# TensorE's program as a loop over heads, with K and V rings of one head each, in a single-query attention kernel

## The chip, the cores and the metric

One core of a Trainium2 chip. The metric is device time in microseconds (us), the median of several executions. The kernel before takes 336.5 us. "Span" is the profiled execution from its first to its last instruction; the times are 1.7 to 2.6 us longer.

## The reference

Attention of one query per head over a long sequence: 16 heads, 8192 keys, head size 256, bfloat16.

```python
B, H, Sq, Sk, D = 1, 16, 1, 8192, 256
scores = jnp.einsum("bhqd,bhkd->bhqk", q, k) * D ** -0.5
p = softmax(scores)
out = jnp.einsum("bhqk,bhkd->bhqd", p, v)
```

K and V are 134 MB and are read once. One head's K is loaded in two halves of 2 MB (32 columns of 128 keys each), and so is its V.

## The kernel before

SyncE issues all loads. K halves go to a ring of 6 buffers, V halves to a ring of 4. Of the 32 columns of a K half, VectorE multiplies 24 with the query (one multiply-and-sum each); TensorE transposes and multiplies the other 8. After a head's two K halves VectorE finds the maximum, ScalarE computes the exponents E, and TensorE multiplies E with V ("PV", 16 matmuls per V half).

The order of the loads: four K halves first, then V and K in turn, so the last K half is followed by four V halves.

```python
items = [("k", *kx) for kx in kseq[:K_LEAD]]            # K_LEAD = 4
rest_k, vseq = kseq[K_LEAD:], list(kseq)
while rest_k or vseq:
    if vseq:   items.append(("v", *vseq.pop(0)))
    if rest_k: items.append(("k", *rest_k.pop(0)))
# [cut] each load waits until its buffer is free:
if n >= slots:                                          # 6 for K, 4 for V
    waits = [f"{kind}free{n - slots}"] + ([f"ktfree{n - slots}"] if kind == "k" else [])
```

A K buffer is free when VectorE has done its 24 columns (`kfree`) and TensorE its 8 (`ktfree`); a V buffer when its PV is done (`vfree`). VectorE does the global maximum of the head before (`xmax`) after the tenth column of the next head's first K half, so E and PV of a head come only then:

```python
for n, (h, x) in enumerate(kseq):
    for c in range(DVE_COLS):                           # 24
        dve(... tensor_tensor_reduce(prod, Kb[slot][c], qb[h], accum_out=S[:, col]) ...)
        if x == 0 and h >= 1 and c == 9: xmax(h - 1)
        if x == 1 and h >= 1 and c == 9: rcp(h - 1)
    if x == 1: dve(... m[h] = max(S of head h) ...)
```

Every engine's program is emitted straight, 16 heads one after the other. Nine tiny loads named `scr`, before the last V half, are a measuring aid; nobody reads what they load.

## Time and profile before

| | before |
|---|---|
| time, median (range) | 336.5 us (336.39 to 336.52, 3 runs) |
| span | 334.8 us |
| DMA, slices 2 to 37 of 40 | 90% or more busy |
| VectorE, one K half | 8.7 us |
| DMA, one half | 4.9 us |
| one head: DMA / VectorE | 19.6 us / 17.4 us |

From the page of the kernel before: the span; the busy tenths of DMA in 40 slices of the span and the GB/s in each; the DMA queues that carry instructions (packets, MB, share of 16 engines' span); the loads with the median time from issue to landing.

```profile
span 334.8 us, 5443 instructions
...
DMA  7999999999999999999999999999999999999910
GB/s 255 430 429 429 430 425 426 429 429 422 431 427 419 433 431 424 425 431 424 423 435 428 423 427 430 423 427 432 425 423 432 431 419 430 433 419 425 377 66 12
...
q8 instruction: 13, 0.21, 0.3%
q14 instruction: 16, 0.13, 0.1%
...
Kb<-in_k_dram SPq DMA_DIRECT2D x31, 2048.0 KB, 39.0
Vb<-in_v_dram SPq DMA_DIRECT2D x31, 2048.0 KB, 34.4
...
```

DMA has 9 in nearly every slice, near 430 GB/s (419 to 435 from the second to the 37th): it bounds the kernel. A load lands 34 to 39 us after its issue, so seven or eight are queued at any time. The page also lists two queues of kind "instruction": q8 with 13 packets of 16,384 bytes, which took 0.98 to 1.11 us each, and q14 with 16 packets.

The trace holds more. In it each load's semaphore gets 16 increments, one by one: those of the last K half come from 296.98 to 309.83 us. They are read here as 16 parts of the load, and "ring" is the name given to what brings one part. Worked out from those moments for the kernel before (us; "step" is the time from the last increment of the load before):

```
load              1st ring   15th ring   16th (last)   step of last
k half  ..           96.36       99.07       100.40        4.89
  ..                101.24      103.97       106.31        5.91
  ..                106.18      108.86       111.16        4.85
  ..                120.86      124.51       125.85        4.86
  ..                130.60      134.29       136.61        5.87
last K half         296.98      301.24       309.83        5.84
V half 28           301.87      306.12       314.77        4.95
V half 30           311.64      315.95       324.51        4.83
```

The first ring keeps a step of about 4.89 us throughout. The last one has a step of 5.7 to 5.9 eleven times between 55 and 310 us and so ends 12.9 us behind the first and 8.6 behind the fifteenth. (The trace doesn't name the rings: 1st to 16th is the order in which they arrive. That the 16th is one and the same ring is inferred from its lag behind the first, which grows step by step; at 208 us it is already 5.3 us behind the fifteenth.) The engines start with the 16th increment: V half 28 has it at 314.77 and its PV starts at 314.82, V half 30 at 324.51 and 324.56. So the last ring sets the time of everything.

TensorE's timeline at the end (start, duration, operation, [idle before it]):

```profile
...
314.82 5.23 PE L471 MATMUL acc<-Vb,E 128*2 128x512 bf16 x16 [0.82 <-DMA Vb<-in_v_dram]
319.88 0.38 PE L413 MATMUL misc<-ident,m 128*1 128x128 f32 x2
320.10 1.89 PE L471 MATMUL acc<-Vb,E 128*2 128x512 bf16 x8
...
322.23 1.89 PE L471 MATMUL acc<-Vb,E 128*2 128x512 bf16 x8
...
324.56 1.03 PE L471 MATMUL acc<-Vb,E 128*1 128x256 bf16 x8 [0.41 <-DMA Vb<-in_v_dram]
...
326.47 6.28 PE L471 MATMUL acc<-Vb,E 128*1 128x256 bf16 x56
```

PV of V half 28 (314.82), the maximum of the last head (319.88), two parts of PV 29 with the last head's softmax between, and then PV 30 and 31 in single rows (324.56 to 332.8).

### The profile page before, as it was taken

The page shows a single profiled execution, that of the slowest core. Times are in us where ns is not written, and L with a number is a line of the kernel's source. Part 1 is how long each engine was busy: PE and PEld are TensorE (multiplying, and loading weights), DVE is VectorE, ACT ScalarE, POOL GpSimd, SP SyncE. Part 2 cuts the span into 40 slices and gives each one's busy share as a digit, 9 for nine tenths or more (in the row PEclk, how much of TensorE's full clock was granted, in tenths as well). Part 3 has the DMA queues.
Part 4 walks back from the last instruction along what each step waited for, and adds up shares of the span by engine and source line. Part 5 has one row for each costly group of instructions (what it writes and reads, how often), then busy time and mean ns, then how long its engine had stood idle before and what let it go on. Part 6 is the DMA issues. An engine that isn't in the chain of part 4 may idle for free.

```text
span 334.8 us, 5443 instructions
## 1 busy us (share of the span) xinstructions
PE 246.3 (74%) x1742; PEld 112.2 (34%) x1742; DVE 281.6 (84%) x1619; ACT 94.3 (28%) x170; POOL 0.2 (0%) x4
## 2 busy tenths in 40 slices
PE   1455857877887877697778688777788776887797
PEld 0433323333332423333233232333333333332335
DVE  7799999799998989787899797998787989797910
ACT  2253204333231324313143321333213333221310
POOL 0000000000000000000000000000000000000000
PEclk9999969799877969869698987779877789877799
DMA  7999999999999999999999999999999999999910
GB/s 255 430 429 429 430 425 426 429 429 422 431 427 419 433 431 424 425 431 424 423 435 428 423 427 430 423 427 432 425 423 432 431 419 430 433 419 425 377 66 12
DMA packets 10289, 134.59 MB, mean 402 GB/s; under 512 B 1282, under 2 KB 1299, under 8 KB 2068
## 3 DMA queue, kind: packets, MB, share of 16 engines
q1 hardware_dynamic: 10224, 134.23, 95.0%
q8 instruction: 13, 0.21, 0.3%
q14 instruction: 16, 0.13, 0.1%
q10 hardware_dynamic: 36, 0.02, 0.0%
HBM read 134.23 MB, written 0.01 MB: 401 GB/s over the span
## 4 chain that ended last, share of the span: by engine, by line
DMA 56%; PE 22%; DVE 16%; ACT 4%; issue 1%; SPq 1%; DVEq 0%
DMA Vb<-in_v_dram 29%; DMA Kb<-in_k_dram 27%; PE acc L471 18%; DVE prod L265 15%; ACT KT L372 2%; PE acc L492 2%; PE tp L363 1%; ACT ac L486 1%; SPq L227 1%; PE misc L423 1%; ACT E L437 1%; DVE S L265 0%; PE spe L388 0%; DVE g L239 0%; PE tp L316 0%
## 5 line engine op out<-in xcount | busy, mean ns | idle before, releaser
L265 DVE CUSTOM_DVE_ANT_0 prod<-Kb,qb 128x256 bf16<-128x256 bf16 x768 | 269.6, 413 | 33.1 <-DMA Kb<-in_k_dram 33.0
L471 PE MATMUL acc<-Vb,E 128*2 128x512 bf16 (+1 forms) x544 | 157.9, 459 | 4.1 <-DMA Vb<-in_v_dram 4.0
L372 ACT ACTIVATE KT<-tp 128x1024 bf16<-128x1024 bf16 x64 | 62.0, 1021 | 107.0 <-PE tp L363 107.0
L471 PEld LDWEIGHTS acc<-Vb,E 128*2 128x2 bf16 (+1 forms) x544 | 51.6, 99 | 97.1 <-issue 63.1
L265 DVE DVE_READ_ACCUMULATOR2_ANT S<- 128x1 f32 x768 | 57.7, 75 | 0.0
L363 PE MATMUL tp<-identb,Kb 128*128 128x128 bf16 x512 | 37.4, 231 | 11.2 <-DMA Kb<-in_k_dram 11.2
L388 PE MATMUL spe<-qT,KT 128*128 128x1 bf16 x512 | 22.4, 165 | 31.6 <-ACT KT L372 31.6
L363 PEld LDWEIGHTS tp<-identb,Kb 128*128 128x128 bf16 x512 | 31.6, 104 | 24.8 <-issue 14.7
L388 PEld LDWEIGHTS spe<-qT,KT 128*128 128x128 bf16 x512 | 17.0, 97 | 41.9 <-ACT KT L372 41.2
L486 ACT ACTIVATE ac<-acc 2x512 f32<-2x512 f32 x15 | 8.8, 586 | 78.2 <-PE acc L471 77.0
L492 PE MATMUL acc<-ac,w 2*1 2x256 f32 x60 | 15.3, 373 | 9.5 <-ACT ac L486 9.5
L423 PE MATMUL misc<-g,ones_row 1*128 1x1 f32 x32 | 6.6, 272 | 11.8 <-DVE g L239 11.8
L430 ACT ACTIVATE negb<-misc 128x1 f32<-128x1 f32 x16 | 2.7, 171 | 34.5 <-PE misc L423 34.5
L451 PE MATMUL misc<-ones_col,lsum 128*2 128x1 f32 x32 | 3.0, 164 | 11.0 <-ACT E L437 11.0
L492 PEld LDWEIGHTS acc<-ac,w 2*1 2x1 f32 x60 | 3.5, 77 | 20.9 <-ACT ac L486 16.6
L423 PEld LDWEIGHTS misc<-g,ones_row 1*128 1x128 f32 x32 | 5.2, 202 | 13.4 <-DVE g L239 12.9
L413 PE MATMUL misc<-ident,m 128*1 128x128 f32 x32 | 6.3, 278 | 3.6 <-DVE m L284 3.6
L239 DVE TENSOR_REDUCE g<-misc 1x1 f32<-1x128 f32 x16 | 4.4, 275 | 3.9 <-PE misc L413 3.9
L507 ACT ACTIVATE o<-acc 1x256 bf16<-1x256 f32 x15 | 5.4, 357 | 1.8 <-PE acc L492 1.8
L437 ACT ACTIVATE E<-S,negb 128x64 bf16<-128x64 f32 x16 | 5.6, 348 | 0.5
L451 PEld LDWEIGHTS misc<-ones_col,lsum 128*2 128x2 f32 x32 | 1.5, 82 | 12.6 <-ACT E L437 12.3
L324 ACT ACTIVATE qb<-tp 128x512 bf16<-128x512 f32 (+1 forms) x9 | 4.9, 549 | 2.5 <-PE tp L316 1.9
(29 smaller groups left out, 27.2 us busy)
## 6 DMA issues: line engine op xcount, KB each, us to landing
Kb<-in_k_dram SPq DMA_DIRECT2D x31, 2048.0 KB, 39.0
Vb<-in_v_dram SPq DMA_DIRECT2D x31, 2048.0 KB, 34.4
Kb<-in_k_dram SPq DMA_DIRECT2D x1, 1024.0 KB, 8.3
Vb<-in_v_dram SPq DMA_DIRECT2D x1, 1024.0 KB, 18.1
Kb<-in_k_dram SPq DMA_DIRECT2D x2, 256.0 KB, 2.8
Kb<-in_k_dram SPq DMA_DIRECT2D x1, 512.0 KB, 6.3
Vb<-in_v_dram SPq DMA_DIRECT2D x1, 512.0 KB, 18.9
Vb<-in_v_dram SPq DMA_DIRECT2D x2, 256.0 KB, 19.2
```

Of the source, the lines that this page charges most:

```text
L265: lambda e, slot=slot, c=c, col=col, h=h, r=(ttr - 1) % PROD: e.tensor_tensor_reduce(out=prod[:, r * D : (r + 1) * D], in0=Kb[slot][:, c * ...
L324: lambda e: e.activation(out=qb[:, a * D : b * D], in_=bank[:, 0 : (b - a) * D], func=ACT.Copy),
L363: lambda e, c=c, hf=hf, i=(b * NH + hf) * P, view=view: e.transpose(view[:, i : i + P], Kb[slot][:, c * D + hf * P : c * D + (hf + 1) * P] ...
L372: lambda e, gn=gn, view=view: e.activation(out=KT[gn % KT_SLOTS][:, :], in_=view[:, 0 : GROUP * D], func=ACT.Copy),
L388: lambda e, b=b, hf=hf, oc=oc, gn=gn: e.matmul(spe[h % 2][:, oc : oc + 1], lhsT=KT[gn % KT_SLOTS][:, (b * NH + hf) * P : (b * NH + hf + 1) ...
L413: lambda e: e.matmul(misc[s][0:1, MT0 : MT0 + P], lhsT=m[:, h : h + 1], rhs=ident[:, :], start=True, stop=True),
L423: lambda e: e.matmul(misc[s][:, BC0 : BC0 + 1], lhsT=ones_row[0:1, :], rhs=g[0:1, h : h + 1], start=True, stop=True),
L437: lambda e: e.activation(out=E[:, h * J : (h + 1) * J], in_=S[:, h * J : (h + 1) * J], func=ACT.Exp, bias=negb[:, h : h + 1], scale=SCALE, ...
L471: lambda e, c=c, col=col: e.matmul(a[0:step, 0 : step * D], lhsT=E[:, col : col + step], rhs=Vb[slot][:, c * D : (c + step) * D], start=(x ...
L486: lambda e: e.activation(out=ac[s][:, :], in_=acc[s][0:2, :], func=ACT.Copy),
L492: lambda e, i=i: e.matmul(acc[s][0:1, 0:D], lhsT=w2[0:2, 2 * h + i : 2 * h + i + 1], rhs=ac[s][0:2, i * D : (i + 1) * D], start=(i == 0), ...
L507: lambda e: e.activation(out=o[0:1, h * D : (h + 1) * D], in_=acc[s][0:1, 0:D], func=ACT.Copy),
```

## The change

Its intent: TensorE's straight program has 3,484 matmuls and weight loads (1,742 each on the page), and the 13 packets of q8 are taken for the fetches of its instructions. If heads 1 to 14 are a loop with a body of about 217 instructions, most of those packets should go. The body is emitted once, with the buffers of its first head, so every ring must hold exactly one head: 2 K halves and 2 V halves. Semaphores are waited for against registers that grow per turn. With two V slots V must also follow K more closely, so the order of the loads is new. The `scr` loads go.

```diff
-K_SLOTS = 6
-V_SLOTS = 4
+UNROLL = 1
+K_SLOTS = 2 * UNROLL
+V_SLOTS = 2 * UNROLL
-K_LEAD = 4
+LAGS = (1, 2, 3) if UNROLL == 1 else (3, 3, 4)
+LAG_AT = 8
@@ TensorE's emitter [cut before and after]
+            with nc.Fori(0, n, 1, engines=[eng.engine], head_slot={eng.engine: 0}):
+                for j in range(step):
+                    for s, v, d in waits[j]:
+                        eng.wait_ge(s, regs[(v, d)] if d else v)
+                    self.run("pe", eng, self.bodies[0] + j)
+                for (v, d), r in regs.items():
+                    eng.reg_add(r, r, d)
@@ order of the loads
-        items = [("k", *kx) for kx in kseq[:K_LEAD]]     [cut]
+        lag = [(0, LAGS[0])] + [(n, LAGS[1]) for n in (LAG_AT,)] + [(NIT - 1, LAGS[2])]
+        for n, kx in enumerate(kseq):
+            items.append(("k", *kx))
+            want = [b for a, b in lag if a <= n][-1]
+            while nv <= n - want:
+                items.append(("v", *kseq[nv])); nv += 1
@@ TensorE's program, one turn [lines joined, loads of the queries cut]
+        for h in range(H - 1):
+            if h and (h - 1) % UNROLL == 0: plan.mark()
+            if h: softmax(h - 1)
+            k_turn(2 * h)
+            if h: softmax2(h - 1)
+            k_score(2 * h)
+            if h: lmm(h - 1); pv(2 * (h - 1))
+            k_turn(2 * h + 1); k_score(2 * h + 1)
+            if h: pv(2 * (h - 1) + 1); merge(h - 1); final(h - 1)
@@ the last head [cut before]
+        k_turn(n + 1); k_score(n + 1)
+        pv(n - 2)
+        softmax(H - 1)
+        pv(n - 1, 0, HALF // 2); softmax2(H - 1); pv(n - 1, HALF // 2, HALF)   [cut]
```

So V trails K by one half for the first eight K halves, by two after that, and three V halves follow the last K half. The broadcasts of all queries are now done during head 0, and E, the maximum and some small tiles have one or two slots instead of 16.

## The prediction

> **What bounds it now.** Core span 334.8 us. The page's slices show DMA at 90% or more from slice 2 to 37, at 420 to 430 GB/s: 2 MB per 4.9 us, 19.6 us a head. VectorE needs 8.7 us per K half (24 columns, 0.345 us apart, timeline); TensorE has idle time. So DMA bounds it, and the landings show which part: a transfer lands with 16 increments, and the last falls behind the fifteenth: 2 us at 100 us, 5.2 at 208, 8.6 at the end (324.51 against 315.95). It loses about 1 us at each of TensorE's 13 instruction fetches (DMA table and packets: 16 KB, about 1.07 us each, some 21 us apart). One ring carries them all. [...]
>
> **Removed.** About 12 of 13 fetches: the late ring joins the others, and transfers land some 8 us earlier at the end.
>
> **What of it reaches the end.** The end hangs on the last K half: before, it lands at 309.83 and the span ends 25 us later (8.9 us of columns and maximum, softmax between halves of PV, then 64 single-row matmuls, output). Now three V halves follow the last K, not four, so K comes one place later; at the fifteenth increment's pace that place lands at 306.1. The 8 us shrink to about 4: span 330.5 if DMA never idles.
>
> **Added.** Rings shrink from 6+4 to 2+2 halves. First data needs about 1.6 us after an issue on an idle queue.
> - From the ninth K half on, V trails K by two halves. A K slot is free 8.7 us after its landing; its reload's turn comes 14.7 us after it. Slack 3.9 us after latency; V has about 7. No gap.
> - Before that V trails by one. Its reload waits for the PV of two halves earlier, which starts only after the maximum (3.75 us into the next K half) and exponent (1.5 us more) and takes 5.2 us (6.2 early): done 10.2 us or more after that K's landing, while the transfers already issued are all landed at 9.8. With the latency a gap of 2.2 to 3.3 us per head for heads 1 to 3, and 1 us at the change of lag. Estimate 8 to 10 us.
> - Back edge: [...] No trace of before shows it.
>
> Sum: 330.5 + 8 = 338.5 of span; the time is 1.7 us above the span: 340, shaded to 339.
>
> **Predicted** 339 us, range 330 to 346. Faster by over 2%: 0.10; within: 0.71; slower: 0.19.
>
> **What would show each step.** TensorE's instruction packets 13 to 1-3. Last increment within 2 us of the fifteenth at the end. DMA slices of 7 or 8 tenths between 35 and 95 us, 9 after. Landings of one head 22 us apart early, 19.6 later. SyncE waiting for PV early. Last K landing near 314, end 24 to 25 us later.
>
> **What would make it wrong.** Early gaps smaller than worked out (then 332 to 335); the loop refetching its block each turn (fetches stay, or TensorE stalls, well above 346); rings unable to run ahead of each other with two slots, so that the other engines' fetches add up.

## More of the kernel before

SyncE's waits before (who waited for whom: us in total, times, longest):

```profile
...
SPq L227 <- PE acc L471: 261.2, 28, 14.8
...
SPq L227 <- DVE S L265: 1.5, 2, 1.1
...
```

## The result

| | before | after |
|---|---|---|
| time, median (range) | 336.51 us (336.39 to 337.36, 4 runs) | 358.53 us (357.86 to 361.16, 4 runs) |
| ratio, 95% interval | 1 | 1.0663 (1.0607 to 1.072) |
| span | 334.8 | 357.1 |
| packets on q8 / q14 | 13 / 16 | 3 / 16 |
| last K half landed | 309.83 | 327.25 |
| from there to the end | 25.0 | 29.8 |

A ratio here is the mean time of one kernel's fast runs over the mean of the other's in the same rounds, so it is not quite the ratio of the medians. The change makes the kernel 6.6% slower, outside the predicted range of 330 to 346.

The same lines of the page after the change:

```profile
span 357.1 us, 5551 instructions
...
DMA  7996995995999999999999999999999999996290
GB/s 277 428 428 281 362 428 215 434 435 213 441 378 417 430 439 417 436 426 428 432 415 433 396 407 374 431 400 368 431 422 425 425 415 372 423 411 291 83 387 7
...
q14 instruction: 16, 0.13, 0.1%
q8 instruction: 3, 0.05, 0.1%
...
Kb<-in_k_dram SPq DMA_DIRECT2D x31, 2048.0 KB, 11.7
Vb<-in_v_dram SPq DMA_DIRECT2D x31, 2048.0 KB, 14.6
...
```

Ten of the 13 packets of q8 are gone, as the change wanted. But DMA has slices of 5 and 6 up to the tenth slice and of 6 and 2 near the end, and a load now lands 12 to 15 us after its issue: the queue is two or three loads deep. SyncE's waits after:

```profile
...
SPq L306 <- DVE S L348: 154.6, 27, 7.7
SPq L306 <- PE acc L577: 104.9, 22, 19.8
...
```

It now waits longest for VectorE, whose columns free the K slots; before, it waited almost only for PV, with some seven loads still queued.

**The early gaps.** Worked out from the 16 increments (us), the loads after the change, up to 100 us, whose last ring has a step over 8 us, and what ended the wait of their issue:

```
load        issued   1st ring   15th ring   last    step of last   PV that freed the slot ends
V half 2     35.49      42.40       42.82   43.80       9.19            35.46
V half 4     59.61      66.40       66.73   66.75       8.28            59.6
V half 6     83.39      90.28       90.57   90.58       8.46            83.4
```

SyncE's timeline after the change (start, duration), and TensorE's for the same time:

```profile
...
23.17 0.33 SPq L306 DMA_DIRECT2D Kb<-in_k_dram  x1
35.49 0.33 SPq L306 DMA_DIRECT2D Vb<-in_v_dram  x1
35.86 0.43 SPq L306 DMA_DIRECT2D Kb<-in_k_dram  x1
...
```

```profile
...
28.16 0.58 PE L528 MATMUL misc<-g,ones_row 1*128 1x1 f32 x2 [1.81 <-DVE g L319]
...
29.58 5.88 PE L577 MATMUL acc<-Vb,E 128*2 128x512 bf16 x16
35.39 1.07 PE L461 MATMUL tp<-identb,Kb 128*128 128x128 bf16 x16
...
```

The global maximum of head 0 comes at 28.16, PV of V half 0 runs from 29.58 to 35.46, and V half 2, which needs that slot, is issued at 35.49, with the next K half stuck behind it at 35.86. The load before it had landed at 34.62. Nothing was queued, and the next increments come at 42.40.

**The late reloads.** TensorE's end after the change:

```profile
...
327.30 1.89 PE L461 MATMUL tp<-identb,Kb 128*128 128x128 bf16 x16 [5.66 <-DMA Kb<-in_k_dram]
...
330.67 5.52 PE L577 MATMUL acc<-Vb,E 128*2 128x512 bf16 x16
336.39 0.38 PE L518 MATMUL misc<-ident,m 128*1 128x128 f32 x2 [0.20 <-DVE m L367]
336.61 1.89 PE L577 MATMUL acc<-Vb,E 128*2 128x512 bf16 x8
...
338.73 1.89 PE L577 MATMUL acc<-Vb,E 128*2 128x512 bf16 x8
...
343.50 1.03 PE L577 MATMUL acc<-Vb,E 128*1 128x256 bf16 x8 [2.85 <-DMA Vb<-in_v_dram]
...
345.96 9.03 PE L577 MATMUL acc<-Vb,E 128*1 128x256 bf16 x56
```

PV of V half 28 (330.67) stands behind the last K half's work (327.30) in TensorE's program. It ends at 336.2, and V half 30 needs its slot: it is issued at 336.23 and landed at 343.46, so TensorE waits 2.85 us for it at 343.50, and the rows that took 6.28 us for 56 before take 9.03. Before, V half 30 was issued at 299.54, 10.3 us ahead of the last K half's landing; now it is 9.0 us behind it.

### The profile page after: what moved, and what is told of

Same layout as the page of the kernel before. It is cut to its first block, busy times and chain, and to the rows that moved or that the text cites. A ratio compares the mean times of both kernels' runs of the same rounds, so it can differ in the third digit from the quotient of the medians.

```text
span 357.1 us, 5551 instructions
## 1 busy us (share of the span) xinstructions
PE 250.3 (70%) x1742; PEld 117.0 (33%) x1742; DVE 282.0 (79%) x1619; ACT 96.8 (27%) x186; POOL 0.2 (0%) x4
## 4 chain that ended last, share of the span: by engine, by line
DMA 53%; DVE 32%; PE 11%; issue 2%; ACT 1%; SPq 1%; DVEq 0%
DMA Kb<-in_k_dram 51%; DVE prod L348 30%; PE acc L577 9%; DMA Vb<-in_v_dram 2%; DVE S L348 1%; DVE w L329 1%; SPq L306 1%; ACT KT L470 1%; PE misc L528 0%; PE acc L599 0%; ACT E L542 0%; PE tp L461 0%; DVE recip L327 0%; DVE g L319 0%; PE misc L557 0%
## 5 line engine op out<-in xcount | busy, mean ns | idle before, releaser
L461 PE MATMUL tp<-identb,Kb 128*128 128x128 bf16 x512 | 40.7, 243 | 25.8 <-DMA Kb<-in_k_dram 25.8
L461 PEld LDWEIGHTS tp<-identb,Kb 128*128 128x128 bf16 x512 | 34.6, 109 | 36.6 <-issue 27.8
L487 PE MATMUL spe<-qcur,KT 128*128 128x1 bf16 x512 | 21.1, 166 | 21.5 <-ACT KT L470 21.5
L487 PEld LDWEIGHTS spe<-qcur,KT 128*128 128x128 bf16 x512 | 16.7, 99 | 26.8 <-ACT KT L470 26.5
L599 PE MATMUL acc<-ac,w 2*1 2x256 f32 x60 | 15.8, 383 | 9.5 <-ACT ac L592 9.5
L327 DVE RECIPROCAL recip<-misc 2x1 f32<-2x1 f32 x16 | 2.4, 150 | 3.6 <-PE misc L557 3.6
L500 ACT ACTIVATE S<-spe 128x16 f32<-128x16 f32 x16 | 2.9, 183 | 7.2 <-PE spe L487 7.2
```

The lines of the kernel that those rows point to most:

```text
L461: lambda e, c=c, hf=hf, i=(b * NH + hf) * P, view=view: e.transpose(view[:, i : i + P], Kb[slot][:, c * D + hf * P : c * D + (hf + 1) * P] ...
L487: lambda e, b=b, hf=hf, oc=oc, gn=gn: e.matmul(spe[sl(h)][:, oc : oc + 1], lhsT=KT[gn % KT_SLOTS][:, (b * NH + hf) * P : (b * NH + hf + 1) ...
L599: lambda e, i=i: e.matmul(acc[s][0:1, 0:D], lhsT=w2[0:2, 2 * s + i : 2 * s + i + 1], rhs=ac[s][0:2, i * D : (i + 1) * D], start=(i == 0), ...
```

## The experiments

Twelve kernels ran, all with correct results. Each line of the table is against the kernel before in the same rounds.

| run | median us | ratio (95%) |
|---|---|---|
| straight, no loop | 357.91 | 1.0624 (1.0596 to 1.0652) |
| lag of two from the start | 349.46 | 1.0405 (1.0347 to 1.0464) |
| straight, V ring of 4 | 341.84 | 1.0166 (1.0130 to 1.0201) |
| straight, K ring 6, V ring 4 | 340.50 | 1.0106 (1.0086 to 1.0126) |
| bodies of two heads | 341.65 | 1.0150 (1.0133 to 1.0167) |
| lag of two, end reordered | 341.34 | 1.0121 (1.0081 to 1.0161) |
| the same, VectorE looped too | 331.79 | 0.9862 (0.9824 to 0.9901) |
| before, no-ops on VectorE | 336.76 | 0.9998 (0.9977 to 1.0020) |
| before, no-ops on TensorE | 336.59 | 0.9997 (0.9973 to 1.0020) |
| before, more VectorE instructions | 339.18 | 1.0077 (1.0060 to 1.0094) |
| before, more TensorE instructions | 336.74 | 1.0015 (0.9989 to 1.0040) |
| before, six K halves first | 336.89 | 1.0020 (0.9994 to 1.0046) |

### 1. Is it the loop? The changed kernel, straight

```diff
-        loop = self.bodies if e == "pe" else []
+        loop = []
```

> The changed kernel with TensorE's program emitted straight, no loop; rings, order and lags as changed. Ring theory (the loss is the small rings; TensorE's fetches are not on the ring that lands last): 13 fetches return, the time stays within 2 us of the changed kernel's 358.5, the last ring's lag grows 1 us at each of VectorE's fetches only. Loop theory (the back edge costs TensorE time): 350 us or less. Fetch theory of the prediction (TensorE's fetches make the last ring late): about 366 us.

From its page:

```profile
...
q8 instruction: 13, 0.21, 0.2%
q14 instruction: 16, 0.13, 0.1%
...
```

All 13 packets of q8 are back and the time is the same within the spread of the runs, 357.9 us against 358.5. The loop itself neither costs nor gains. In particular the last ring got nothing from the absence of TensorE's fetches: in both kernels its steps of 5.7 to 6.2 us between 115 and 330 us come at a packet of q14. In the changed kernel q14 has packets at 119.9, 147.0, 170.6, 197.3, 221.1, 249.9, 273.4, 299.9 and 324.0, and the last ring has its long steps at 122.4, 152.8, 173.3, 198.8, 224.8, 255.5, 276.1, 301.8 and 327.3. Three more packets of q14, at 103.9, 278.2 and 303.8, are off this beat and meet no such step; for which engine they are, the trace doesn't say. The kernel before shows the same: each of its eleven long steps ends within 6 us of a packet of q14. One step of the straight kernel may be TensorE's: 6.81 us at 111.6 has a packet of q8 (107.9) in it, where the change of lag had let the rings run dry (5.49 at the same place with the loop); it doesn't show in the time. The regular packets of q14 carry VectorE's instructions (experiment 6). The step on which the prediction rested, that TensorE's fetches make the last ring late, had matched packets to steps by their rough spacing only. In the kernel before both queues have one of about 24 us (q8 from 28.1 to 316.4 and q14's regular packets from 14.8 to 306.5, each in twelve intervals).

### 2. The early gaps: V two halves behind from the start

```diff
-LAGS = (1, 2, 3) if UNROLL == 1 else (3, 3, 4)
+LAGS = (2, 2, 3) if UNROLL == 1 else (3, 3, 4)
```

> The changed kernel with V trailing K by two halves from the start instead of one for the first eight. Theory (V's reload waits for the PV of the head before, and the queue runs dry): the steps of 8 to 9 us between landings before 92 us go, only one or two of about 1 us stay; 348 us (346 to 351). Rival (the early gaps are absorbed by later slack, or come from the start of the loop): within 3 us of 358.5.

The steps over 8 us are gone (the longest before the last three V halves is 7.21, at 32 us), the last K half lands at 317.04 instead of 327.25, and the time falls by 9 us. The early gaps are real, they reach the end, and the lag of one made them.

### 3. Which ring: V ring of 4; K ring of 6 and V ring of 4

Both straight, since a loop body of one head can't have them.

```diff
-V_SLOTS = 2 * UNROLL
+V_SLOTS = 4
```

> Straight, K ring 2, V ring 4, lags as changed (1, 2, 3). Theory (V's ring of two made both the early gaps, 12 us, and the late reloads of the last two V halves, 5 us): about 341 us. Rival (K's ring of two is too small because the late ring holds back every landing): 350 us or more.

```diff
-K_SLOTS = 2 * UNROLL
-V_SLOTS = 2 * UNROLL
+K_SLOTS = 6
+V_SLOTS = 4
```

> Straight, rings of before (K 6, V 4), the changed kernel's order and lags. Theory: no gaps; the last K half has one place later in the stream than before (4.9 us), so about 341 us, same as with K 2 and V 4. Rival (the order and single buffers of the changed kernel cost by themselves): 345 us or more.

Both as expected: 341.8 and 340.5 us. Against the straight kernel of experiment 1, two more V slots take 16 us away (357.9 to 341.8), by both effects, the early gaps (the last K half lands at 316.18, 9.5 us earlier) and the late reloads (the end follows after 23.5 us, 6.7 us sooner). Four more K slots on top bring 1.3 us. With all rings as before, the last K half lands at 314.57, which is one place (4.9 us) later than before, and the end follows 24.1 us after it. So a ring of two is long enough for K to within 1.3 us, as predicted. The 3.7 us that remain go with the new order and with the single buffers of the other tiles; this run doesn't separate the two.

### 4. The changed program with bodies of two heads

```diff
-UNROLL = 1
+UNROLL = 2
```

> The changed program with bodies of two heads [...]and so rings of 4 and 4, lags 3, 3, 4 as it has them. Theory (the rings of one head were the cost): no early gaps, late V reloads free, last K half near 310, 336 to 338 us. Rival (a loop on TensorE costs by itself[...]): fetches at every turn in TensorE's queue and 342 us or more.

341.65 us, a miss of the size and not in the way the rival has it. q8 has 4 packets in the whole run, so a body of two heads (about 434 instructions, at 217 a head) is not fetched again at its seven turns. The early gaps are gone and the last K half lands at 308.8. But the end comes 30.9 us later. From the waits of this run, and of the kernel before, the line in which VectorE waits for TensorE's transpose of the maxima:

```profile
...
DVE g L319 <- PE misc L518: 35.2, 15, 4.8
...
```

```profile
...
DVE g L239 <- PE misc L413: 3.9, 3, 2.0
...
```

VectorE stands still for 35 us in 15 heads before the global maximum, up to 4.8 us each time. In the changed order that transpose comes after the PV of the second V half and its merge; with a lag of 3 to 4 halves TensorE first waits for that V half. VectorE starts on the last K half at 314.67, 5.9 us after its landing (0.1 us after it in the kernel before), and that is the whole difference between 30.9 and 25.0 us. That cause is read from the waits and the timeline; no run isolates it.

### 5. The end of the changed kernel, reordered

On top of experiment 2:

```diff
         lmm(H - 2)
+        pv(n - 2)
         k_turn(n + 1)
         k_score(n + 1)
-        pv(n - 2)
+        pv(n - 1)
         softmax(H - 1)
-        pv(n - 1, 0, HALF // 2)
-        softmax2(H - 1)
-        pv(n - 1, HALF // 2, HALF)
-        lmm(H - 1)
-        pv(n, 0, HALF // 4)
         merge(H - 2)
         final(H - 2)
+        softmax2(H - 1)
+        lmm(H - 1)
+        pv(n, 0, HALF // 4)
```

> The changed kernel, loop and rings of one head kept, V two halves behind from the start, and TensorE's last head reordered so that the two V slots come free before the last K half's work instead of after it. Theory: last K half lands near 317 as with the lag alone, the end follows 22 to 24 us later instead of 29; 343 us (341 to 346). Rival (the end hangs on the softmax of the last head alone): within 2 us of 349.5.

341.34 us: 8 us less than with the lag alone. The end now follows 22.1 us after the last K half (318.00 to 340.1), against 29.1 with the lag alone. V half 30 is issued at 317.63 instead of 326.87. The late reloads were a second cost of their own, caused by the place of the last PVs in TensorE's program. (The run moves two PVs and the merge at once; what each is worth isn't separated.) With both mended, loop and rings of one head are within 1.2% of the kernel before.

### 6. Whose fetches make the last ring late?

First two builds that put instructions without effect among VectorE's columns (336 of them) and among TensorE's PV matmuls (1344). The edit on VectorE, and then on TensorE:

```diff
+                if h < H - 2 and c % 2 == 1:
+                    dve(lambda e: e.nop())
```

> The kernel before with 336 instructions that do nothing put among VectorE's columns (one after every second column, heads 0 to 13)[...]. Theory (each fetch of VectorE's stops one ring for about 1 us, and that ring lands last): 2 or 3 more packets in VectorE's instruction queue, the last ring 2 to 3 us later at the end, 339.4 us (338.5 to 340.5). Rival (that ring is slow for another reason): within 0.7 us of before, 336.8.

```diff
+                if h < H - 2:
+                    for _ in range(3):
+                        pe(lambda e: e.nop())
```

> The kernel before with 1344 instructions that do nothing put among TensorE's PV matmuls (three after each, heads 0 to 13)[...]. Prediction's theory (TensorE's fetches make the last ring late): 5 us more, 341.5. Theory now (they fall on other rings, which are 8 us ahead of the last): within 1 us of before, with 18 packets in TensorE's instruction queue.

Neither moved the time, and neither tells anything: both profiles still have 5443 instructions and 13 and 16 packets. The no-ops never reached the chip's program. A test that adds a cost must show in the profile that the cost is there. So they were repeated with real work that nobody reads, memsets of one element and matmuls of zeros:

```diff
@@ among VectorE's columns [the new tile xs cut]
+                if h < H - 2 and c >= 10:
+                    dve(lambda e, i=ttr: e.memset(xs[0:1, i % 512 : i % 512 + 1], 0.0))
```

> The kernel before with 392 one-element memsets that nobody reads put among VectorE's columns (14 per K half, heads 0 to 13), in place of the instructions without effect, which the build had dropped[...]. Theory (each VectorE fetch stops the ring that lands last for about 1 us): 3 more packets in VectorE's queue, last K half at about 312.8 instead of 309.8, 339.8 us (339 to 341). Rival (VectorE's fetches only coincide with a slow ring): the last ring's lag at the end stays 12 to 13 us and the time within 1 us of before.

```profile
...
q8 instruction: 13, 0.21, 0.3%
q14 instruction: 19, 0.16, 0.1%
...
```

```diff
@@ among the PV matmuls [lines joined, the new tile zb cut]
+                if h < H - 2 and c < HALF - step:
+                    pe(lambda e: e.matmul(a[0:2, 0:1], lhsT=zb[:, 0:2], rhs=identb[:, 0:1],
+                                          start=False, stop=False), None, ["c_zb", "c_id"])
```

> The kernel before with 420 one-column matmuls of zeros (840 instructions with their weight loads) put among the PV matmuls of heads 0 to 13[...]. Prediction's theory (TensorE's fetches make the last ring late): 3 us more, 340. Theory now: 3 more packets in TensorE's queue, each 0.4 to 1 us on one of the other rings, the last ring as before, time within 1 us of before.

```profile
...
q8 instruction: 17, 0.28, 0.3%
q14 instruction: 16, 0.13, 0.1%
...
```

392 more VectorE instructions give three more packets on q14, the last K half lands 2.35 us later (312.18), and the time is 2.4 us longer. In that run the last ring has 14 long steps instead of 11 and at the last K half lands 15.8 us behind the first instead of 12.9, while the other fifteen are not later (the fifteenth at 300.43 against 301.24), so it isn't VectorE's added work that delays the loads. 840 more TensorE instructions give four more packets on q8 and no change of the time; the last ring stays 12.9 us behind the first. So q14's regular packets are VectorE's, one per some 130 instructions (392 for three more; 1,619 for 13 regular ones in the kernel before), and q8's are TensorE's, one per 210 to 270 (840 for four more; 3,484 for 13). VectorE's set the last ring back by about 1 us: in the kernel before each of its 11 long steps (5.7 to 5.9 us instead of 4.9) comes at one of the 13 regular packets. TensorE's don't show in the last ring. The one at 120.0 in the kernel before meets a step of 5.87 of the fifteenth increment, which ends at 124.51, and of 4.86 of the last; the fifteenth has time to spare (8.6 us at the end). For the rest the trace doesn't say on which ring they fall.

### 7. VectorE's program as a loop too

If that is so, the loop belongs on VectorE. On top of experiment 5: the loop emitter serves VectorE as well, heads 1 to 14 are one body, scores S have one buffer that is copied when a head is done, and ScalarE copies the head's query to a fixed place, one copy per K half so that none is waited for.

```diff
-                        in1=qb[:, h * D : (h + 1) * D],
+                        in1=qc2[x][:, :] if h else qb[:, 0:D],
@@ at the start of a head, and [cut] at its end, before the maximum [lines joined]
+            if x == 0 and h >= 1:
+                plan.mark("dve")
             if x == 1:
+                dve(lambda e: e.tensor_copy(S2[:, :], S[:, :]), f"cp{h}", [...])
@@ the emitter [cut]
-        loop = self.bodies if e == "pe" else []
+        loop = self.bodies.get(e, [])
```

> As the run with lag and end mended, and VectorE's program for heads 1 to 14 a loop body of one head too (scores copied at the head's end, q copied per half by ScalarE). Theory (VectorE's fetches stop the ring that lands last): its instruction packets after the start fall from 13 to 3 or fewer, the last increment stays within 2 us of the fifteenth, the last K half lands 8 us earlier, near 308; 333 us (331 to 337), below before. Rival (that ring is slow by itself, or the loop refetches): the same as without this loop, 343 us, or slower.

```profile
span 329.3 us, 5703 instructions
...
DMA  7899999999999999999999999999999999999973
GB/s 285 350 412 411 370 426 430 428 435 426 430 424 434 422 432 426 430 428 430 430 428 430 428 430 426 428 428 432 424 429 427 432 428 430 428 426 425 360 299 123
...
q8 instruction: 3, 0.05, 0.1%
q14 instruction: 6, 0.05, 0.0%
...
```

331.79 us, 1.4% faster than the kernel before: q14 has 6 packets instead of 16 (3 or fewer of VectorE's own were expected; the page doesn't say which of the 6 are), the slices from the sixth to the 37th are near 430 GB/s, and the last K half lands at 308.43 instead of 318.00, with an expectation of 308. Between 50 and 300 us no load's last ring has a step over 5.0 us; the next long one, 6.12 at 303.5, has a packet of q14 at 302.5. Besides fetches this run changed copies and buffers, but those add work; together with the dose test of experiment 6 it settles whose fetches cost.

### 8. What does the end of the kernel before hang on?

```diff
-K_LEAD = 4
+K_LEAD = 6
```

> The kernel before with six K halves ahead of the first V instead of four. Theory (its end hangs on the last K half): that lands two places, 9.8 us, earlier, near 300, and the end hangs on the last V half instead, 330.0 plus 3 to 4 us: 335 us (334 to 336). Rival (the end hangs on the last landing already): within 0.5 us of before.

The rival is right: the last K half lands 10 us earlier (299.47) and the time does not move (336.9 us). From TensorE's timeline of that run:

```profile
...
324.35 1.03 PE L471 MATMUL acc<-Vb,E 128*1 128x256 bf16 x8 [1.11 <-DMA Vb<-in_v_dram]
...
326.26 6.27 PE L471 MATMUL acc<-Vb,E 128*1 128x256 bf16 x56
```

PV of V half 30 starts when it has landed, at 324.35 (324.56 in the kernel before), and the remaining rows take 10.3 us from there to the end in both. In the kernel before TensorE waits 0.41 us for V half 30, so the chain from the last K half is ready only that much earlier: two chains end almost together, and V half 30 ends last. The prediction saw only the first.

## Why the prediction was wrong

The prediction was 338.5 us of span (shaded to a time of 339); the span is 357.1, so 18.6 us were missed. The last K half was to land at 314 and landed at 327.25 (13.2 us); the end was to follow 24.4 us later and followed after 29.8 (5.4 us). The 24.4 are its sum 330.5 less its 306.1.

| step, as the prediction put it | predicted | measured | us missed |
|---|---|---|---|
| "the late ring joins the others, and transfers land some 8 us earlier" | last K half at 306.1 without gaps | its place in the stream of before lands at 314.77 with the last ring, and that ring was not relieved | 8.7 |
| early gaps "8 to 10 us" (8 in the sum) | 8 | 327.25 less 314.77 = 12.5 (11.1 of it by K half 10, at 111.49; that place landed at 100.40 before) | 4.5 |
| "end 24 to 25 us later" | 24.4 | 29.8 | 5.4 |

- **The failed step is the first.** "One ring carries them all" was said of TensorE's fetches. That one ring is late is right; that TensorE's fetches make it late is wrong. Experiments 1, 6 and 7 show that they are VectorE's. The change removed ten fetches that cost nothing (experiment 1). The gain of 8 us that the prediction set against the smaller rings didn't exist.
- **The early gaps: mechanism right, size too small.** Place, cause and timing were as predicted (V's reload waiting for the PV of two halves earlier; one head in 23 to 24 us; PV ends 10.9 to 11.1 us after the K half's landing, "10.2 us or more" in the prediction). The term that was most mis-sized is the restart of an idle queue, "about 1.6 us". Less the 4.89 us of moving, the first increment of V halves 4 and 6 comes 1.9 and 2.0 us after their issue and the last one 2.2 and 2.3 us. At V half 2 they come after 2.0 and 3.4 us; a packet of q14 (40.7) falls into that load. The 1.6 us agrees with the first increment at the start of the kernel before: 256 KB, issued at 0.74, has it at 2.90, and less the 0.61 us that 256 KB take at 430 GB/s that is 1.55; its last one, at 3.40, makes 2.05.
- **The end: a wait overlooked.** The prediction counted three V halves behind the last K half as if they streamed. With two slots V half 30 waits for the PV of V half 28, which the new program puts behind the last K half's work. Experiment 5 shows the cost: 8 us with the lag mended. Its premise, "the end hangs on the last K half", was wrong for the kernel before as well: there V half 30 ends last (experiment 8).
- **Right:** the steady state with a lag of two has no gaps of its own (experiment 2, from 40 us to the last K half: steps of 4.9 us, and of the longer ones all but one of 5.28 at a packet of q14); a K ring of two is enough to within 1.3 us (experiment 3); the loop body is not fetched again (3 packets on q8, and 4 with a body of two heads, experiment 4), and the back edge costs nothing that the time shows (experiment 1: 358.5 us with the loop, 357.9 without).
- **A sign that told nothing.** The prediction offered "last increment within 2 us of the fifteenth at the end" as proof that the late ring is relieved. After the change the two are 2.9 us apart at the last K half instead of 8.6, which looks like most of the way, and yet the ring was not relieved: with two slots the leading rings have no work to run ahead with, so they wait for the last (the first ring's steps after 200 us are up to 6.2 us; in the kernel before at most 5.0). The step of the last ring is the measure, not its distance.

From 336.5 to 358.5 us, by the runs: 9 us are the early gaps (experiment 2), 8 us the late reloads (experiment 5), and the remaining 4.6 us are a difference that no run takes apart: they go with the last K half's later place in the stream (4.9 us in experiment 3) and small gaps, less an end that is now shorter. The gain that was there to be had, 9.5 us between experiments 5 and 7, was in another engine's instructions.

## What to carry to other kernels

Where the increments of a load come far apart (12.9 us at the end of the kernel before), read them ring by ring and match each long step to one packet before naming its cause; two queues with nearly the same period (about 24 us here) look alike. Here a ring of two V halves was too short where the consumer's freeing point, in its program order, came after the queue had run dry (V half 2 issued at 35.49, the load before landed at 34.62): work that out at the start and the end, where the order differs, and not only in the steady state. If a loop is to save instruction fetches, put it on the engine whose fetches hold back the last ring: here VectorE (9.5 us between experiments 5 and 7), not TensorE (experiment 1).
